# Broadcast of the reciprocal denominators in four transfers, three denominators computed inside the first gate/up, a third x1 buffer

## The chip, the cores and the metric

The kernel runs on one core of a Trainium2 chip, in one launch. The metric is the device time of one execution in microseconds, from three runs: median 884.3 us (880.92 to 885.51). A lower time is better. The profile shows one execution in detail: PE is TensorE (matmul; PEld is its weight load), DVE is VectorE, ACT is ScalarE, POOL is GpSimd, SP is SyncE, which here only issues DMAs.

## The reference

A transformer block in bf16 with S = 2048 tokens and D = 1024 features, conditioned by a vector c. `silu(c) @ w_mod` gives six vectors of 1024: shift, scale and gate for each of the two halves.

```python
h = layernorm(x) * (1 + ca) + sa
x = x + ga * A(h)             # linear attention, 32 heads of 32
h = layernorm(x) * (1 + cb) + sb
x = x + gb * B(h)             # silu(h @ w_gate) * (h @ w_up) @ w_down, F = 3584

# A: q, k, v = h @ wqkv
pq, pk = phi(q), phi(k)       # phi(t) = (t + 1 if t > 0 else exp(t)) + 1e-6
kv  = einsum('bhsd,bhse->bhde', pk, v);  z = sum of pk over s
num = einsum('bhqd,bhde->bhqe', pq, kv)
den = einsum('bhqd,bhd->bhq', pq, z) + 1e-6
A   = (num / den) @ wo
```

Because `kv` and `z` are sums over all tokens, no query can be finished before the keys of all tokens are done.

## The kernel before

The tokens are worked off in four chunks of 512 (`sc` = 0 to 3), each of four tiles of 128 rows. Features lie on the 128 partitions in eight groups of four heads (`hg`), so that q of one chunk is eight blocks of 128 x 512 (`q_phase(sc, lo, hi)`, one block `qc` each: eight matmuls into one accumulator, then `phi_to`: an Exp on ScalarE, L260, and two VectorE instructions, L261 and L262). The four accumulators `acc` (pool `pa`) are shared by q, k, v, gate/up and down.

The stages in order are: the first layer norm and k, v for all chunks, with q of chunk 0; then `kv` is masked to its head blocks and transposed (L471 to L481), and `wo` is multiplied by it in place (L485 to L492), so that later `pq @ wo` gives the attention output directly, provided that `pq` has been divided by its denominator. Between these stand the remaining q blocks. Then the four tiles of chunk 0 go through `wo_tile`, the q blocks that remain are done, and for each chunk follow `gate_up` (seven blocks `fb` of two 1 MB weight tiles `wgu`, four `f` each) and `down` (eight groups of 28 matmuls). `down` of chunk sc has the four `wo_tile` of chunk sc + 1 between its groups.

The denominators go through two functions. `den_norm(sc)` multiplies `pq` by `Zden` (32 small matmuls, L366 to L369), adds an epsilon and takes the reciprocal on VectorE (L371, L374), writes the 128 x 128 result to a DRAM scratch `rden_scratch` in four writes, two from ScalarE's queue and two from GpSimd's (L377), and reads it back from GpSimd's queue into the 1 MB tile `rbc`, each head's row copied to that head's 32 partitions (L380). `den_apply(sc)` multiplies `pq` by `rbc` in four VectorE instructions of two head groups (L388).

`wo_tile(st)` (L496 to L525) makes one tile of the residual stream x1: two halves of eight matmuls each (`a_ps`), the residual add (L513) and statistics (L514) on VectorE, a store of x1 to a DRAM scratch from ScalarE's queue (L515), rstd and a shift on GpSimd (L192, L206), the normalise on ScalarE (L208), and a transposing DMA from SP into `h2T` (L523). The fourth tile of a chunk is followed by eight `modulate` instructions on VectorE (L211). `down` loads x1 back in halves, `x1r`, from SP (L563), multiplies by the gate (L569), adds (L571) and stores (L572).

Who comes first on an engine is set by a planner that orders the traced instructions by its own estimates, with these exceptions: matmuls keep the order of the text (`keep_in_program_order`), and instructions under `tc.issue_after(i)` are queued on i's engine behind i (issue order only, no wait for i to finish). Every engine and every DMA queue works in order. SBUF tiles come from pools: a tile named in a pool of n buffers waits for the release of the one n before it; pool `k8` has 19 buffers of 8 KB per partition, which `rbc`, `wgu`, `wd`, `gu`, `pq`, `h2T`, `wq` and others share. Pool `x1p` holds two `x1` (4 KB) and three `x1r` (2 KB), pool `ep` three `e` (2 KB, used by gate/up and down) and three `eb`.

Of the kernel before, what the change touches and what calls it, by code (L numbers as in the profile page):

```python
# [9 lines left out]
ALU = mybir.AluOpType  # L10
BF16 = mybir.dt.bfloat16
F32 = mybir.dt.float32
# [9 lines left out]
def kernel(  # L22
# [13 lines left out]
    nc = tc.nc  # L36
    P = nc.NUM_PARTITIONS
    _, S, D = A_x.shape
    F = B_w_gate.shape[1]
    DH = 32  # L40
    HPC = P // DH
    ST = S // P
    DC = D // P
    HG = DC
    FC = F // P
    SCW = 512
    NSC = S // SCW
    STC = SCW // P
    NB = 512
# [19 lines left out]
    const = ctx.enter_context(tc.tile_pool(name="const", bufs=1))  # L69
    dram = ctx.enter_context(tc.tile_pool(name="dram", bufs=1, space=DRAM))  # L70
    k8 = ctx.enter_context(tc.tile_pool(name="k8", bufs=19))
    k2 = ctx.enter_context(tc.tile_pool(name="k2", bufs=5))
    x1p = ctx.enter_context(tc.tile_pool(name="x1p", bufs=2))
    ep = ctx.enter_context(tc.tile_pool(name="ep", bufs=3))
    yp = ctx.enter_context(tc.tile_pool(name="yp", bufs=2))
    small = ctx.enter_context(tc.tile_pool(name="small", bufs=4))
# [20 lines left out]
    def mm(out, lhsT, rhs, start, stop):  # L97
        return tc.keep_in_program_order(nc.tensor.matmul(out, lhsT=lhsT, rhs=rhs, start=start, stop=stop))  # L98
# [4 lines left out]
    def big(name, shape):  # L103
        return k8.tile([P] + shape, BF16, name=name, tag="k8")

    def acc_a():
        return pa.tile([P, NB], F32, name="acc", tag="pa")
# [21 lines left out]
    for b in range(2):  # L129
        ts = []  # L130
        for q in (1, 0):
            t = big("wme", [DC, NB])
# [31 lines left out]
    ca1T = const.tile([P, DC], F32, name="ca1T")  # L164
    sbT = const.tile([P, DC], F32, name="sbT")
    cb1T = const.tile([P, DC], F32, name="cb1T")
    ga_bc = const.tile([P, D], BF16, name="ga_bc")
    gb_bc = const.tile([P, D], BF16, name="gb_bc")
    kvs = k8.tile([P, HG * VW + HG * P], F32, name="kvs", tag="k8")
    kv_acc = kvs[:, 0:HG * VW].rearrange("p (g e) -> p g e", e=VW)  # L170
# [73 lines left out]
    def mod_block(b, q):  # L244
# [10 lines left out]
        else:  # L255
            nc.vector.tensor_copy(out=saT[:, cs], in_=src)

    def phi_to(dst, acc):
        e = ep.tile([P, NB], BF16, name="eb")
        nc.scalar.activation(out=e[:], in_=acc, func=ACT.Exp)  # L260
        nc.vector.tensor_scalar(out=e[:], in0=e[:], scalar1=1.0, scalar2=PHI_EPS, op0=ALU.min, op1=ALU.add)  # L261
        nc.vector.scalar_tensor_tensor(out=dst, in0=acc, scalar=0.0, in1=e[:], op0=ALU.max, op1=ALU.add)  # L262

    pks, vs, pqs = {}, {}, {}

# [33 lines left out]
    def q_phase(sc, lo=0, hi=DC):  # L299
        if lo == 0:  # L300
            pqs[sc] = big("pq", [HG, SCW])
        for qc in range(lo, hi):
            acc = acc_a()
            for cc in range(DC):
                mm(acc[:], lhsT=wq[cc // 4][:, cc % 4, qc * P:(qc + 1) * P], rhs=hTs[sc][:, cc, :],
                                 start=(cc == 0), stop=(cc == DC - 1))
            phi_to(pqs[sc][:, qc, :], acc[:])
# [55 lines left out]
    def den_norm(sc):  # L363
        pq = pqs[sc]
        den = acc_b("den")
        for hg in range(HG):  # L366
            for q in range(STC):
                mm(den[32 * q:32 * q + 32, 0:P], lhsT=Zden[:, hg, :], rhs=pq[:, hg, q * P:(q + 1) * P],
                                 start=(hg == 0), stop=(hg == HG - 1))  # L369
        dsum = small.tile([P, P], F32, name="dsum", bufs=2)  # L370
        nc.vector.tensor_scalar_add(out=dsum[:], in0=den[:, 0:P], scalar1=DEN_EPS)  # L371
        rb = small.tile([P, P], BF16, name="rb", bufs=2)
        with nc.allow_low_precision("bf16 reciprocal multiplies bf16 phi(q)"):
            nc.vector.reciprocal(out=rb[:], in_=dsum[:])  # L374
        for q in range(STC):
            eng = nc.gpsimd if q % 2 else nc.scalar
            eng.dma_start(out=rden_dram[sc, :, q * P:(q + 1) * P], in_=rb[32 * q:32 * q + 32, :])  # L377
        rbc = big("rbc", [HG, SCW])
        rv = rden_dram[sc].rearrange("(h g) t -> h (g t)", h=HPC)
        nc.gpsimd.dma_start(out=rbc[:].rearrange("p g t -> p (g t)"),  # L380
                            in_=rv.unsqueeze(1).to_broadcast([HPC, DH, HG * SCW]))
        rbcs[sc] = rbc

    def den_apply(sc):
        pq, rbc = pqs[sc], rbcs.pop(sc)
        for k in range(4):
            ks = slice(2 * k, 2 * k + 2)
            nc.vector.tensor_tensor(out=pq[:, ks, :], in0=pq[:, ks, :], in1=rbc[:, ks, :], op=ALU.mult)  # L388
# [51 lines left out]
    for sc in range(NSC):  # L440
        if sc > 0:
            k_phase(sc, 0, 2)
            kv_phase(sc - 1)
            if sc == 2:
                mod_bc(row)
            if sc == 3:
                mod_cols(row)
            k_phase(sc, 2, 8)
        v_phase(sc)
        if sc + 1 < NSC:  # L450
            with tc.issue_after(last_on[nc.vector.engine]):
                ln1(sc + 1)
                modulate_all(hTs[sc + 1], ca1T, saT)
        if sc == 0:
            q_phase(0)
        if sc + 2 < NSC:
            for st in range((sc + 2) * STC, (sc + 3) * STC):
                load_x(st, nc.sync)
        if sc == 1:
            row = mod_rows([2 * D, 2 * D + NB, 5 * D, 5 * D + NB])  # L460
        if sc == 2:
            row = mod_rows([3 * D, 3 * D + NB, 4 * D, 4 * D + NB])
            wo = load_w(wo_v, 0, "wo")
            for cc in range(DC):
                w = wo[cc // 4][:, cc % 4, :]
                nc.vector.tensor_tensor(out=w, in0=w, in1=ga_bc[:], op=ALU.mult)

    q_phase(1, 0, 2)
    kv_phase(NSC - 1)
    for h in range(2):  # L470
        hs = slice(4 * h, 4 * h + 4)  # L471
        nc.vector.tensor_tensor(out=KVZ[:, hs, :], in0=kv_acc[:, hs, 0:P],
                                in1=kvmask[:].unsqueeze(1).to_broadcast([P, 4, P]), op=ALU.mult)
        nc.vector.tensor_tensor(out=Zden[:, hs, :], in0=kv_acc[:, hs, P:P + 1].to_broadcast([P, 4, DH]),
                                in1=zmask[:, hs, :], op=ALU.mult)
# [4 lines left out]
    nc.scalar.copy(out=KVT[:, 0:4, :], in_=tpk[:, 0:4, :])  # L480
    nc.vector.tensor_copy(out=KVT[:, 4:8, :], in_=tpk[:, 4:8, :])  # L481
    den_norm(0)
    den_apply(0)
    q_phase(1, 4, 5)
    wf = [(hg, nb) for hg in range(HG) for nb in range(NNB)]  # L485
    for qc in range(5, 11):
        q_phase(1 + qc // 8, qc % 8, qc % 8 + 1)
        for hg, nb in wf[3 * (qc - 5):3 * (qc - 4)]:
            ps = acc_b("wf")
            w = wo[hg // 4][:, hg % 4, nb * NB:(nb + 1) * NB]  # L490
# [40 lines left out]
    def gate_up(sc, between=None):  # L531
        guT[sc] = []
        for fb in range(NFB):
            wb = []
            for view in (wg_v, wu_v):
                w = big("wgu", [DC, FBW])
                last_w[sc] = nc.sync.dma_start(out=w[:], in_=view[:, :, fb * FBW:(fb + 1) * FBW])
                wb.append(w)
            for fj in range(FPB):
                f = fb * FPB + fj  # L540
                if f % GPT == 0:
                    guT[sc].append(big("gu", [min(GPT, FC - f), SCW]))
                ps = []
                for w in wb:
                    acc = acc_a()
                    for cc in range(DC):
                        last_mm[sc] = mm(acc[:], lhsT=w[:, cc, fj * P:(fj + 1) * P], rhs=h2Ts[sc][:, cc, :],
                                              start=(cc == 0), stop=(cc == DC - 1))
                    ps.append(acc)
                sg = ep.tile([P, NB], F32, name="e")  # L550
                nc.scalar.activation(out=sg[:], in_=ps[0][:], func=ACT.Silu)  # L551
                gm = nc.vector.tensor_tensor(out=guT[sc][f // GPT][:, f % GPT, :], in0=ps[1][:], in1=sg[:], op=ALU.mult)  # L552
            if between and fb in between:
                with tc.issue_after(gm.ins):
                    between[fb]()

    def down(sc, side):
        for t in range(STC):
            st = sc * STC + t
            for nb in range(NNB):  # L560
                ns = slice(nb * NB, (nb + 1) * NB)
                x1r = x1p.tile([P, NB], F32, name="x1r", bufs=3)
                nc.sync.dma_start(out=x1r[:], in_=x1_dram[st * P:(st + 1) * P, ns])  # L563
                y_ps = acc_a()
                for f in range(FC):
                    mm(y_ps[:], lhsT=guT[sc][f // GPT][:, f % GPT, t * P:(t + 1) * P],
                                     rhs=wd[f // WDF][:, f % WDF, ns], start=(f == 0), stop=(f == FC - 1))
                yt = ep.tile([P, NB], F32, name="e")
                nc.vector.tensor_tensor(out=yt[:], in0=y_ps[:], in1=gb_bc[:, ns], op=ALU.mult)  # L569
                ob = yp.tile([P, NB], BF16, name="ob")  # L570
                nc.vector.tensor_tensor(out=ob[:], in0=yt[:], in1=x1r[:], op=ALU.add)  # L571
                nc.sync.dma_start(out=out2[st * P:(st + 1) * P, ns], in_=ob[:])  # L572
                if side:
                    with tc.issue_after(last_mm[sc].ins):
                        side.pop(0)()

    q_phase(2, 3, 4)
    den_norm(1)
    q_phase(2, 4, 5)
    for st in range(STC):  # L580
        wo_tile(st)
    q_phase(2, 5, 8)
    q_phase(3, 0, 5)
    den_norm(2)
    q_phase(3, 5, 8)
    def late_den():
        den_apply(2)
        den_norm(3)

    gate_up(0, {2: lambda: den_apply(1), 3: late_den, 5: lambda: den_apply(3)})  # L590
    wd = []
    for b in range(FC // WDF):
        w = big("wd", [WDF, D])
# [38 lines left out]
```

## Time and profile before

| | |
|---|---|
| median of three runs | 884.3 us |
| lowest, highest | 880.92, 885.51 us |
| profiled execution, time | 881.36 us |
| its span, first to last instruction | 879.6 us |
| TensorE busy | 840.3 us (96%) |
| VectorE, ScalarE, GpSimd busy | 306.7, 173.9, 37.0 us |
| mean granted TensorE clock | 0.986 of full |

The span is the time from the first to the last instruction of the profiled execution; its own time is 1.8 us more. The page has a strip in which each digit is the busy share of one of forty equal slices of 22 us. The chain of waits follows the last instruction back, step by step, to what released it. In the timeline a bracket behind an instruction gives the idle time before it on its engine and what ended it. Times "to landing" of a DMA run from its issue to its completion. A busy TensorE need not run at full clock: the granted clock of a stretch is given as a share of full speed.

### The profile page before, as it was taken

The page shows a single profiled execution, that of the slowest core. Times are in us where ns is not written, and L with a number is a line of the kernel's source. Part 1 is how long each engine was busy: PE and PEld are TensorE (multiplying, and loading weights), DVE is VectorE, ACT ScalarE, POOL GpSimd, SP SyncE. Part 2 cuts the span into 40 slices and gives each one's busy share as a digit, 9 for nine tenths or more (in the row PEclk, how much of TensorE's full clock was granted, in tenths as well). Part 3 has the DMA queues.
Part 4 walks back from the last instruction along what each step waited for, and adds up shares of the span by engine and source line. Part 5 has one row for each costly group of instructions (what it writes and reads, how often), then busy time and mean ns, then how long its engine had stood idle before and what let it go on. Part 6 is the DMA issues. An engine that isn't in the chain of part 4 may idle for free.

```text
span 879.6 us, 10369 instructions
## 1 busy us (share of the span) xinstructions
PE 840.3 (96%) x4201; PEld 387.4 (44%) x4284; DVE 306.7 (35%) x602; ACT 173.9 (20%) x267; POOL 37.0 (4%) x124
## 2 busy tenths in 40 slices
PE   9989999959599998999999999999999999999997
PEld 4434445524244443444444444444444444444443
DVE  5776334426531422443121134321212441212122
ACT  1555333342221121110111101011111101111100
POOL 2120000001000000000000000000000000000000
PEclk9999999989799999999999999999999999999999
DMA  9779530017995497552744226294321737820021
GB/s 298 288 156 296 182 121 1 2 49 96 251 296 160 145 185 237 171 150 91 222 142 138 103 80 216 69 289 135 121 96 42 216 91 247 267 96 1 7 66 36
DMA packets 127311, 128.74 MB, mean 146 GB/s; under 512 B 34976, under 2 KB 108832, under 8 KB 126752
## 3 DMA queue, kind: packets, MB, share of 16 engines
q1 hardware_dynamic: 122208, 115.36, 45.7%
q10 hardware_dynamic: 2688, 8.46, 2.5%
q0 software_dynamic: 2368, 4.27, 2.1%
q8 instruction: 33, 0.54, 0.3%
q14 instruction: 14, 0.11, 0.0%
HBM read 108.01 MB, written 12.71 MB: 137 GB/s over the span
## 4 chain that ended last, share of the span: by engine, by line
PE 82%; DMA 11%; DVE 4%; issue 1%; ACT 1%; POOL 1%; ACTq 0%; SPq 0%; DVEq 0%; POOLq 0%
PE acc L98 75%; DMA rbc<-rden_scratch 5%; PE a_ps L98 5%; DMA x1r<-x_scratch 2%; DMA wd<-in_B_w_down_dram 2%; DVE stats L198 1%; DVE pq L388 1%; DMA x_scratch<-x_2148 1%; DMA x_sb<-in_A_x_dram 1%; PE kvp L98 1%; DMA h2T<-xn 0%; DMA rden_scratch<-rb 0%; PE modr L98 0%; DVE pq L262 0%; ACT v L297 0%
## 5 line engine op out<-in xcount | busy, mean ns | idle before, releaser
L98 PE MATMUL acc<-h2T,wgu 128*128 128x512 bf16 x1757 | 385.9, 379 | 4.6 <-DVE gu L552 2.7
L98 PEld LDWEIGHTS <-wgu 128*128 128x128 bf16 x1792 | 175.3, 98 | 214.1 <-issue 3.0
L98 PE MATMUL acc<-wd,gu 128*128 128x512 bf16 x878 | 195.0, 379 | 3.0 <-DMA wd<-in_B_w_down_dram 2.1
L552 DVE TENSOR_TENSOR gu<-acc,e 128x512 bf16<-128x512 f32 x112 | 77.3, 691 | 294.3 <-PE acc L98 281.7
L551 ACT ACTIVATE e<-acc 128x512 f32<-128x512 f32 x112 | 66.9, 597 | 376.7 <-PE acc L98 358.9
L98 PEld LDWEIGHTS <-gu 128*128 128x128 bf16 x896 | 87.7, 98 | 108.1 <-issue 2.6
L98 PE MATMUL acc<-hT,wq 128*128 128x512 bf16 x248 | 62.3, 403 | 24.1 <-DVE pq L262 23.4
L98 PEld LDWEIGHTS <-hT 128*128 128x128 bf16 x512 | 49.6, 98 | 60.8 <-DVE hT L211 1.0
L569 DVE TENSOR_TENSOR e<-acc,gb_bc 128x512 f32<-128x512 f32 x32 | 22.1, 690 | 121.2 <-PE acc L98 112.8
L98 PE MATMUL a_ps<-wo,pq 128*128 128x512 bf16 x250 | 56.9, 379 | 0.3
L98 PE MATMUL acc<-wk,hT 128*128 128x512 bf16 x250 | 56.1, 379 | 0.3
L98 PE MATMUL acc<-wv,hT 128*128 128x512 bf16 x249 | 55.5, 379 | 0.4
L260 ACT ACTIVATE eb<-acc 128x512 bf16<-128x512 f32 x64 | 37.5, 596 | 75.6 <-PE acc L98 49.7
L98 PEld LDWEIGHTS <-wq 128*128 128x128 bf16 x256 | 26.0, 102 | 57.4 <-issue 31.1
L261 DVE TENSOR_SCALAR eb<-eb 128x512 bf16<-128x512 bf16 x64 | 18.4, 290 | 71.9 <-ACT eb L260 71.7
L98 PEld LDWEIGHTS <-pq 128*128 128x128 bf16 x256 | 25.0, 98 | 30.2
L192 POOL TENSOR_TENSOR rstd<-veps,neg_half 128x1 f32<-128x1 f32 x32 | 17.9, 558 | 449.7 <-DVE veps L190 449.7
L297 ACT CAST v<-acc 128x512 bf16<-128x512 f32 x32 | 18.7, 584 | 31.4 <-PE acc L98 30.3
L198 DVE BATCH_NORM_STATS2 stats<-x_sb 128x6 f32<-128x512 bf16 x32 | 20.6, 672 | 7.7 <-DMA x_sb<-in_A_x_dram 7.5
L571 DVE TENSOR_TENSOR ob<-e,x1r 128x512 bf16<-128x512 f32 x32 | 22.1, 692 | 1.1
L262 DVE SCALAR_TENSOR_TENSOR pk<-acc,eb 128x512 bf16<-128x512 f32 x32 | 22.1, 690 | 0.8
L262 DVE SCALAR_TENSOR_TENSOR pq<-acc,eb 128x512 bf16<-128x512 f32 x32 | 21.8, 686 | 0.7
(116 smaller groups left out, 251.0 us busy)
## 6 DMA issues: line engine op xcount, KB each, us to landing
wgu<-in_B_w_gate_dram SPq DMA_DIRECT2D x28, 1024.0 KB, 7.5
wgu<-in_B_w_up_dram SPq DMA_DIRECT2D x28, 1024.0 KB, 8.2
x_sb<-in_A_x_dram SPq DMA_DIRECT2D x32, 256.0 KB, 5.7
wml<-in_w_mod_dram SPq DMA_DIRECT2D x8, 1024.0 KB, 9.7
x1r<-x_scratch SPq DMA_DIRECT2D x32, 256.0 KB, 3.0
wd<-in_B_w_down_dram SPq DMA_DIRECT2D x7, 1024.0 KB, 28.7
wme<-in_w_mod_dram SPq DMA_DIRECT2D x4, 1024.0 KB, 11.2
rbc<-rden_scratch POOLq DMA_DIRECT2D x4, 1024.0 KB, 23.8
```

Of the source, the lines that this page charges most:

```text
L98: return tc.keep_in_program_order(nc.tensor.matmul(out, lhsT=lhsT, rhs=rhs, start=start, stop=stop))
L192: nc.gpsimd.tensor_tensor(out=rstd[:, 0:n], in0=veps[:, 0:n], in1=neg_half[:].to_broadcast([P, n]), op=ALU.pow)
L198: nc.vector.bn_stats(out=stats[:, i, :], in_=src[:, i * NB:(i + 1) * NB])
L260: nc.scalar.activation(out=e[:], in_=acc, func=ACT.Exp)
L261: nc.vector.tensor_scalar(out=e[:], in0=e[:], scalar1=1.0, scalar2=PHI_EPS, op0=ALU.min, op1=ALU.add)
L262: nc.vector.scalar_tensor_tensor(out=dst, in0=acc, scalar=0.0, in1=e[:], op0=ALU.max, op1=ALU.add)
L297: nc.scalar.copy(out=v[:, t, nb * 4:(nb + 1) * 4, 0:P], in_=acc[:].rearrange("p (g e) -> p g e", e=P))
L388: nc.vector.tensor_tensor(out=pq[:, ks, :], in0=pq[:, ks, :], in1=rbc[:, ks, :], op=ALU.mult)
L551: nc.scalar.activation(out=sg[:], in_=ps[0][:], func=ACT.Silu)
L552: gm = nc.vector.tensor_tensor(out=guT[sc][f // GPT][:, f % GPT, :], in0=ps[1][:], in1=sg[:], op=ALU.mult)
L569: nc.vector.tensor_tensor(out=yt[:], in0=y_ps[:], in1=gb_bc[:, ns], op=ALU.mult)
L571: nc.vector.tensor_tensor(out=ob[:], in0=yt[:], in1=x1r[:], op=ALU.add)
```

## The change

Four things are edited. The read of `rbc` becomes four DMAs of 32 partitions each, one per head of a group. `den_apply(0)` moves from before the wo folding to behind the phi of q block (2, 3), and the norms of chunks 1, 2 and 3 move into the first `gate_up`: norm 1 after block 0, apply 1 and norm 2 after block 2, apply 2 and norm 3 after block 4, apply 3 after block 6, the last. (Before, norm 1 stood after q block (2, 3), norm 2 after (3, 4), apply 1 after block 2, apply 2 and norm 3 after block 3, apply 3 after block 5.) The `x1` tile gets a third buffer and `x1r` gives one up. `ga_bc`, which is used only before the wo folding, lies in one of the three `e` tiles instead of a tile of its own.

```diff
-    x1p = ctx.enter_context(tc.tile_pool(name="x1p", bufs=2))
+    x1p = ctx.enter_context(tc.tile_pool(name="x1p", bufs=3))
...
-    ga_bc = const.tile([P, D], BF16, name="ga_bc")
+    ga_t = ep.tile([P, NB], F32, name="e")
+    ga_bc = ga_t[:].bitcast(BF16)
...
+    last_phi = [None]
+
     def phi_to(dst, acc):
...
-        nc.vector.scalar_tensor_tensor(out=dst, in0=acc, scalar=0.0, in1=e[:], op0=ALU.max, op1=ALU.add)
+        last_phi[0] = nc.vector.scalar_tensor_tensor(out=dst, in0=acc, scalar=0.0, in1=e[:], op0=ALU.max, op1=ALU.add)
...
         rv = rden_dram[sc].rearrange("(h g) t -> h (g t)", h=HPC)
-        nc.gpsimd.dma_start(out=rbc[:].rearrange("p g t -> p (g t)"),
-                            in_=rv.unsqueeze(1).to_broadcast([HPC, DH, HG * SCW]))
+        for h in range(HPC):
+            nc.gpsimd.dma_start(out=rbc[h * DH:(h + 1) * DH].rearrange("p g t -> p (g t)"),
+                                in_=rv[h].unsqueeze(0).to_broadcast([DH, HG * SCW]))
...
     den_norm(0)
-    den_apply(0)
     q_phase(1, 4, 5)
...
-                x1r = x1p.tile([P, NB], F32, name="x1r", bufs=3)
+                x1r = x1p.tile([P, NB], F32, name="x1r", bufs=2)
...
     q_phase(2, 3, 4)
-    den_norm(1)
+    with tc.issue_after(last_phi[0].ins):
+        den_apply(0)
     q_phase(2, 4, 5)
     for st in range(STC):
         wo_tile(st)
     q_phase(2, 5, 8)
-    q_phase(3, 0, 5)
-    den_norm(2)
-    q_phase(3, 5, 8)
-    def late_den():
-        den_apply(2)
-        den_norm(3)
-
-    gate_up(0, {2: lambda: den_apply(1), 3: late_den, 5: lambda: den_apply(3)})
+    q_phase(3)
+
+    def late_den(apply, norm):
+        if apply:
+            den_apply(apply)
+        if norm:
+            den_norm(norm)
+
+    gate_up(0, {0: lambda: den_norm(1), 2: lambda: late_den(1, 2), 4: lambda: late_den(2, 3),
+                6: lambda: den_apply(3)})
```

More of the change, by code (lines that the diff above doesn't have):

```diff
@@ L465 @@
                 w = wo[cc // 4][:, cc % 4, :]
-                nc.vector.tensor_tensor(out=w, in0=w, in1=ga_bc[:], op=ALU.mult)
+                nc.vector.tensor_tensor(out=w, in0=w, in1=ga_bc, op=ALU.mult)
     q_phase(1, 0, 2)
```

## The prediction

> **What bounds the kernel now.** The page's strip of forty slices comes first: it says where TensorE is not busy.
>
> ```profile
> PE   9989999959599998999999999999999999999997
> ```
>
> Two slices of 22 us at 5, the 9th (176 to 198 us) and the 11th (220 to 242), and a small dent in the 16th; everything from 355 us on is full. The busy-time view by stretches prices the gaps:
>
> ```profile
> 187.90:198.40 10.50, 0.10 (x5) 0.12 (x2) 3.50 (x7) 0.01 (x1) 0.00 (x0) 0.63 0.13 37
> 198.35:201.35 3.00, 2.78 (x8) 1.09 (x9) 2.86 (x8) 0.60 (x1) 0.00 (x0) 0.56 0.00 0
> 222.20:230.60 8.40, 0.04 (x2) 0.01 (x1) 3.40 (x9) 2.70 (x4) 0.82 (x2) 0.66 1.02 180
> 230.58:236.42 5.84, 5.83 (x16) 2.06 (x16) 2.64 (x8) 1.20 (x2) 0.00 (x0) 0.61 1.06 314
> 236.40:238.20 1.80, 0.07 (x2) 0.05 (x1) 1.80 (x6) 0.01 (x1) 0.00 (x0) 1.00 1.08 366
> 355.30:870.00 514.70, 512.23 (x2338) 233.30 (x2386) 145.72 (x242) 65.03 (x96) 9.81 (x24) 1.00 0.42 131
> ```
>
> The columns are the stretch, its length, busy time with instruction count of PE, PEld, DVE, ACT and POOL, the granted clock, DMA share and GB/s. After each long gap the clock is about 0.6 for some microseconds. After 355 us nothing is left to gain. So the question is who releases TensorE, which the timeline says at each restart, and the chain says why:
>
> ```profile
> 198.35 0.58 PE L98 MATMUL acc<-hT,wq 128*128 128x512 bf16 x1 [10.40 <-DVE pq L262]
> 230.58 5.83 PE L98 MATMUL acc<-hT,wq 128*128 128x512 bf16 x16 [8.36 <-DVE pq L262]
> 238.15 3.61 PE L98 MATMUL acc<-hT,wq 128*128 128x512 bf16 x16 [1.74 <-DVE pq L262]
> 342.47 5.34 PE L98 MATMUL acc<-h2T,wgu 128*128 128x512 bf16 x24 [2.68 <-DVE gu L552]
> 352.63 1.02 PE L98 MATMUL acc<-wd,gu 128*128 128x512 bf16 x4 [0.50 <-DMA wd<-in_B_w_down_dram]
> 355.22 1.02 PE L98 MATMUL acc<-wd,gu 128*128 128x512 bf16 x4 [1.57 <-DMA wd<-in_B_w_down_dram]
> ```
> ```profile
> 175.51 19.33 DMA rbc<-rden_scratch
> 194.87 2.50 DVE pq L388 x4
> ...
> 205.72 5.85 DMA x_scratch<-x_2148
> 211.59 15.71 DMA x1r<-x_scratch
> ...
> 230.37 4.26 DMA h2T<-xn
> ...
> 310.28 29.02 DMA rbc<-rden_scratch
> ```
>
> First gap: VectorE's four multiplies of `den_apply(0)` stand ahead of the phi work and wait for the 1 MB broadcast; TensorE runs out of its four accumulators. Second gap: ScalarE's queue stands at the fourth x1 store, which waits for an x1r load of 15.71 us, and the Exp work stands behind it. Third: `den_apply(3)` waits for a broadcast of 29.02 us. Why the loads of the second gap are so slow is read from the DMA view of 204 to 232 us, against the same transfers later (400 to 870 us, the last two lines):
>
> ```profile
> rbc<-rden_scratch POOLq DMA_DIRECT2D x1, 1024.0 KB, 22.0
> x1r<-x_scratch SPq DMA_DIRECT2D x3, 256.0 KB, 13.1
> h2T<-xn SPq DMA_TRANSPOSE x4, 8.8
> ...
> x1r<-x_scratch SPq DMA_DIRECT2D x25, 256.0 KB, 3.0
> h2T<-xn SPq DMA_TRANSPOSE x8, 3.3
> ```
>
> Broadcast 1 is in flight beside them for 22.0 us; the loads take 13.1 instead of 3.0, the transposes 8.8 instead of 3.3.
>
> **The change, part by part.** *Four transfers for one broadcast.* In the stretch where broadcast 0 is alone (176.9 to 194.9), the queue table gives
>
> ```profile
> q0 software_dynamic: 465, 1.05, 23.6%
> ```
>
> 23.6% of 16 engines is 3.8 engines at 60 GB/s: the one transfer, whose outermost dimension has four steps, occupies four. Each new one has 32 rows outermost. No row shows such a broadcast, so bounds: from below, a 1 MB weight load lands in 5.1 us at best; from above, the rate stays and three more issues come on top.
>
> ```profile
> L377 POOL DMA_DIRECT2D rden_scratch<-rb x8: 496/503/712, 172.5 to 308.0; - x8
> L380 POOL DMA_DIRECT2D rbc<-rden_scratch x4: 700/710/715, 175.5 to 310.3; - x4
> ...
> DMA to landing us min/median/max: 19.3/23.8/29.0
> ...
> DMA to landing us min/median/max: 5.1/7.9/28.4
> ```
>
> (The landing lines are of the broadcasts and of the weight loads wgu.) An issue costs POOL 0.50 to 0.71 us, so four take 2.0 to 2.8. I take the weight load's median plus three issues: 7.9 + 2.1 = 10.0, landing at 185.5; bounds 175.5 + 5.1 = 180.6 and 175.5 + 19.3 + 2.1 = 196.9. Behind them on POOL stands only the rstd of the first x1 tile, over 10 us later: nothing.
>
> *`den_apply(0)` behind the phi of q(2,3), `den_norm(1)` out of this place.* q(2,3) is the last block before the stall. Its matmuls run 1.89 us from 185.50; then Exp, min and phi, then four multiplies (2.50 us):
>
> ```profile
> 185.50 1.89 PE L98 MATMUL acc<-hT,wq 128*128 128x512 bf16 x8
> ...
> L260 ACT ACTIVATE eb<-acc 128x512 bf16<-128x512 f32 x64 | 37.5, 596 | 75.6 <-PE acc L98 49.7
> L261 DVE TENSOR_SCALAR eb<-eb 128x512 bf16<-128x512 bf16 x64 | 18.4, 290 | 71.9 <-ACT eb L260 71.7
> L262 DVE SCALAR_TENSOR_TENSOR pq<-acc,eb 128x512 bf16<-128x512 f32 x32 | 21.8, 686 | 0.7
> ...
> 356.25 3.45 PE a_ps L98 x16
> ```
>
> 187.4 + 0.6 + 0.3 + 0.7 and hand-overs is 189.1: later than 185.5, so the broadcast is hidden with 3.6 us to spare; without that cover, its lateness comes one to one. The multiplies end at 191.6. TensorE does q(2,4) until 187.4 + 1.7 = 189.1 (sixteen matmuls take 3.45) and then needs the scaled chunk 0. If each pair of head groups is released by its own multiply, the first tile's half ends at 192.0 where 190.8 was possible, 1.2 lost; if it waits for all four, 2.5. Value 1.9, no reason for either. It is shorter than the 2.68 us gap after which the clock stayed whole, so no cold matmuls. Term 1: 10.4, plus the slow clock (8 matmuls in 3.00 us instead of 1.72: 1.3), minus 1.9: **9.8 us**.
>
> *Broadcast 1 and 2 leave the x1 stage, third x1 buffer.* VectorE's longest wait for a free x1 buffer was 6.7 us, ScalarE's wait on the x1r load 10.6:
>
> ```profile
> ACT xn L208 <- DMA x1r<-x_scratch: 10.6, 1, 10.6
> DVE x_2263 L513 <- DMA x_scratch<-x_2187: 6.7, 1, 6.7
> ```
>
> With three buffers, tile 3 takes over the one of tile 0, whose store is issued three tiles (3 x 3.45 us of matmuls) earlier. With no broadcast beside them, loads take 3.0 and transposes 3.3. What is late next: the normalise of tile 3, then Exp of q(2,5). An earlier tile shows its price from the residual add to the end of the normalise, 208.45 to 212.58, 4.1 us:
>
> ```profile
> 208.45 0.69 DVE L513 TENSOR_TENSOR x_2187<-a_ps,x_sb 128x512 f32<-128x512 f32 x1 [0.26 <-PE a_ps L98]
> 211.34 1.24 ACT L208 ACTIVATE xn<-x_2187,nmr,rstd 128x1024 bf16<-128x1024 f32 x1 [2.19 <-POOL nmr L206]
> ```
>
> The eight half tiles end at 192.0 + 7 x 1.73 = 204.1, so Exp of q(2,5) starts at 208.3 and its phi ends at 210.0; four accumulators carry TensorE to 204.1 + 6.9 = 211.0. Covered, by 1.0. The last transpose lands at about 211.8 and the eight modulate instructions may sit ahead of a phi: I leave 0.5, bounds 0 and the present 1.7. Term 2: 8.4 + (5.84 - 3.45) + 1.7 - 0.5 = **12.0 us**.
>
> *Denominators 1 to 3 inside the first gate/up.* Each block of it is 64 matmuls, 13.8 us. Norm and apply now lie two blocks apart, 27.6 us; even the present 24 to 29 us would nearly fit, and 10 to 15 do. Term 3: the third gap, **2.7 us**. The 32 small matmuls of two norms (0.56 us each) move inside; net zero. Each norm puts two writes on ScalarE's queue behind the reciprocal, with SiLU behind them. One such place exists now:
>
> ```profile
> ACT e L551 <- DVE rb L374: 6.4, 1, 6.4
> 300.00:310.00 10.00, 9.95 (x76) 4.58 (x75) 5.14 (x9) 1.79 (x3) 1.00 (x2) 1.00 0.05 9
> ```
>
> SiLU waited 6.4 us and TensorE stayed at 9.95 of 10: the accumulators hide it. Cost 0; if not, 2.7 (the third gap) three times, 8 us.
>
> *`den_apply(3)` at the very end of gate/up.* It frees broadcast 3's buffer later, perhaps for the seventh `wd` load, which TensorE needs 24 matmuls (5.2 us) into the first down group. The last gate weights' buffer falls free 1.7 us before the end, and without a slow broadcast a load lands in 5.1 to 7.9. Of today's 2.1 us of `wd` waits I count half as gone. Term 4: **1.0 us**, bounds 2.1 and, if the load must wait for that buffer (3 us late) and takes 7.9, a loss of 3 + 7.9 - 5.2 - 2.1 = 3.6.
>
> *Two x1r buffers, `ga_bc` in a borrowed tile.* In down a load follows each group's `ob`; with two buffers it has about 10 us until its use and lands in 3.0. The borrowed `e` slot is idle until gate/up. Both 0.
>
> Sum: 9.8 + 12.0 + 2.7 + 1.0 = 25.5 us. The profiled execution took 881.36 us (span 879.6 and 1.8 around it): 855.9. The median of the three runs, 884.3, is 2.9 above the profiled one; I add half of that: **857.4**.
>
> **The rivals.** *A: the four transfers stay as slow as the one.* They are queued one behind the other and read the same 64 KB. For it: 60 GB/s is all the broadcast ever got. Against: 3.8 busy engines explain that rate. Landing 196.9 instead of 189.1 costs 7.8, 1.3 of clock return, the third gap stays: 25.5 - 11.8 = 13.7, so 869.2. The Trainium skill, in SBUF — State Buffer, "Door 1: The DMA port swizzle", says that 32 partitions reach 8 of 16 ports (189 GB/s at 1 MiB), and under "Can I just issue two DMAs to hit both halves?" that two such transfers serialize. By that figure 1 MB takes an estimated 5.5 us, still under the cover; no run here shows it yet, and it keeps A at an eighth.
>
> *B: the second gap moves to the h2T wait.* VectorE stands at the modulate, ahead of phi, while transposes still take 8.8 us, slowed now by stores and weight loads. For it: 4.26 us of the chain is that transfer. Against: 3.3 in every later chunk. Price (8.8 - 3.3) + 2.4 of slow clock: 7.9, so 865.3.
>
> *C: the planner's order undoes it*, the norms landing where VectorE or ScalarE still blocks as long: 884.
>
> *D, slower: x1r becomes the bound.* Its place is every one of the 32 down groups: a load can start only when the `ob` two groups back has ended, in SP's in-order queue behind weight loads. Fully exposed it is 3.0 + 0.4 of issue, 3.4 us a group; half of it is 54 us, 910. It decides from 25.5 / 32 = 0.8 us a group. Against: some 7 us of cover and three spare accumulators.
>
> **How the numbers follow.** Forecast 0.62, A 0.12, B 0.14, C 0.07, D 0.05. Half a percent, 4.4 us, is about what a measurement tells from no change here. Faster holds forecast, A and B, 0.88; C is the same, 0.07; D slower, 0.05. The forecast's own range is 853 (10.4 + 1.3 - 1.2, 12.5, 2.7 and 2.1 make 27.8, so 853.6, and the lowest run shown is 0.4 below the profiled one) to 862 (term 4 at its loss of 3.6). A and B take the range up to 870; at the low end I add 2 for a gap that I did not see.
>
> **What would show it.** Right: each broadcast piece landing within 10 us of the first issue, VectorE at L388 never waiting for it, TensorE's gaps before 230 us under 3 us with clock 1.00 throughout, x1r and h2T near 3 us, gate/up starting some 23 us earlier. Wrong: L388 waiting (A), h2T L211 ahead of a TensorE gap (B), a gap released by SiLU or `wd` in gate/up, or `ob` waiting for x1r (D).

## The result and the profile after

The changed kernel took 857.73 us (median of four runs, 856.37 to 858.9) against 882.61 us for the kernel before on the same chip (four runs, 879.92 to 885.51). The ratio is 0.9717, with a 95% interval from 0.9676 to 0.9758. The profiled execution took 856.37 us with a span of 854.5; the one of before took 881.36, so 25.0 us lie between the two traces.

The strip of TensorE's forty slices, and the granted clock under it, from the page of the changed kernel:

```profile
PE   9989999999999998999999999999999999999997
PEclk9999999999999999999999999999999999999999
```

The two slices at 5 are full. The dents left are the third slice, which was there before as well, and the 16th, and the clock stays at 90% or more in every slice.

The timeline of TensorE at the places where before stood still (start, length, then in brackets the idle time and its releaser):

```profile
189.84 14.50 PE L98 MATMUL a_ps<-wo,pq 128*128 128x512 bf16 x63 [0.61 <-DVE pq L392]
...
215.33 8.79 PE L98 MATMUL acc<-hT,wq 128*128 128x512 bf16 x39 [0.63 <-DVE pq L265]
223.96 13.98 PE L98 MATMUL acc<-h2T,wgu 128*128 128x512 bf16 x63
...
322.66 4.48 PE L98 MATMUL acc<-wd,gu 128*128 128x512 bf16 x20
327.60 0.81 PE L98 MATMUL acc<-wd,gu 128*128 128x512 bf16 x3 [0.46 <-DMA wd<-in_B_w_down_dram]
330.13 1.02 PE L98 MATMUL acc<-wd,gu 128*128 128x512 bf16 x4 [1.73 <-DMA wd<-in_B_w_down_dram]
```

The gaps of 10.4, 8.36 and 1.74 us are now 0.61 and 0.63, and the 2.68 us in gate/up is gone. The waits for `wd` are as long as before, 0.46 + 1.73 = 2.2 against 2.1, but not from the same cause, as shown below.

The same by stretches (stretch, length, busy time of PE, PEld, DVE, ACT, POOL, then clock, DMA share, GB/s): the first gate/up with the start of down, and everything behind the last `wd` wait.

```profile
223.96:327.20 103.24, 102.65 (x555) 46.98 (x564) 31.16 (x49) 18.60 (x30) 8.94 (x18) 1.00 0.71 211
331.16:845.00 513.84, 511.37 (x2335) 232.99 (x2381) 145.87 (x242) 65.04 (x96) 9.81 (x24) 1.00 0.43 132
```

The last row answers the row of before from 355.30 on, 514.70 long with 512.23 busy. The idle rest is 2.47 us in both: nothing was lost or won there. The whole gain lies ahead of it.

The broadcast itself. First VectorE's four multiplies and the issue of broadcast 0 in the timeline, then the broadcast's line with its landing times, over all four broadcasts and for broadcast 0 alone, then its queue in the DMA view of the stretch in which its packets run, 176.8 to 181.2 us:

```profile
175.61 2.00 POOL L384 DMA_DIRECT2D rbc<-rden_scratch  x4 [1.74 <-DMA rden_scratch<-rb]
189.10 2.49 DVE L392 TENSOR_TENSOR pq<-pq,rbc 128x1024 bf16<-128x1024 bf16 x4
```
```profile
L384 POOL DMA_DIRECT2D rbc<-rden_scratch x16: 492/497/539, 175.6 to 303.4; - x16
...
DMA to landing us min/median/max: 3.4/8.9/11.5
...
DMA to landing us min/median/max: 3.4/4.5/6.6
```
```profile
q0 software_dynamic: 175, 1.04, 105.3%
```

The multiplies carry no bracket: they waited for nothing. The four transfers moved 1.04 MB in 4.4 us and held all sixteen engines (packet times overlap, so a share can pass 100%), where the single transfer held 3.8 from 176.9 to 194.9. The last piece landed by 183.7, 6.6 us after its issue.

### The profile page after: what moved, and what is told of

Its sections match the earlier page's. It is cut to its first block, busy times and chain, and to the rows that moved or that the text cites. A ratio compares the mean times of both kernels' runs of the same rounds, so it can differ in the third digit from the quotient of the medians.

```text
span 854.5 us, 10400 instructions
## 1 busy us (share of the span) xinstructions
PE 837.3 (98%) x4201; PEld 386.4 (45%) x4284; DVE 307.5 (36%) x602; ACT 174.1 (20%) x267; POOL 42.1 (5%) x136
## 3 DMA queue, kind: packets, MB, share of 16 engines
q0 software_dynamic: 1024, 4.26, 2.2%
## 4 chain that ended last, share of the span: by engine, by line
PE 91%; DMA 4%; DVE 3%; SPq 1%; issue 1%; ACT 0%; POOL 0%; DVEq 0%; POOLq 0%
PE acc L98 82%; PE a_ps L98 6%; DMA wme<-in_w_mod_dram 2%; DMA wd<-in_B_w_down_dram 1%; DVE stats L199 1%; DMA x_sb<-in_A_x_dram 1%; PE kvp L98 1%; SPq L137 1%; PE modr L98 0%; PE wf L98 0%; DMA h2T<-xn 0%; DVE hT L212 0%; DVE h2T L212 0%; PE den L98 0%; SPq L133 0%
## 5 line engine op out<-in xcount | busy, mean ns | idle before, releaser
L98 PE MATMUL acc<-hT,wq 128*128 128x512 bf16 x249 | 58.5, 387 | 3.9 <-DVE pq L265 3.4
L209 ACT ACTIVATE xn<-x,nmr,rstd 128x1024 bf16<-128x1024 f32 x16 | 19.9, 1241 | 131.3 <-POOL nmr L207 131.3
L516 DVE TENSOR_TENSOR x<-a_ps,x_sb 128x512 f32<-128x512 f32 x32 | 22.1, 691 | 8.3 <-PE a_ps L98 7.6
L517 DVE BATCH_NORM_STATS2 stats<-x 128x6 f32<-128x512 f32 x32 | 22.2, 695 | 1.1
```

The source lines that it names most:

```text
L209: nc.scalar.activation(out=dst, in_=src, func=ACT.Identity, bias=nmr[:], scale=rstd[:, 0:1])
L516: nc.vector.tensor_tensor(out=x1[:, ns], in0=a_ps[:], in1=x_t[:, ns], op=ALU.add)
L517: nc.vector.bn_stats(out=stats[:, nb, :], in_=x1[:, ns])
```

## The experiments

The theory was the prediction's: three gaps, each closed by a part of the change of its own. The first rival gave everything to the split, the second to the order and the buffer. Each ratio below is to the kernel before on the same chip.

**The changed kernel with the single transfer.** The order of the norms and the third buffer stay.

```diff
-        for h in range(HPC):
-            nc.gpsimd.dma_start(out=rbc[h * DH:(h + 1) * DH]..., in_=rv[h].unsqueeze(0)...)
+        nc.gpsimd.dma_start(out=rbc[:]..., in_=rv.unsqueeze(1).to_broadcast([HPC, DH, HG * SCW]))
```

> The changed kernel with the broadcast as one transfer again; everything else as changed. My theory (the split is what makes the broadcast quick, and its lateness comes one to one): broadcast 0 lands near 195 us instead of 184, VectorE waits about 5.7 us at den_apply(0), TensorE loses that and about 1.3 us of slow clock, and the broadcasts inside gate/up take 20 to 29 us again, which costs 0 to 2.5 us at each of the three applies: 865 to 871 us. Rival (the order of the work did it, the split adds little): 857 to 860 us.

Measured: 894.11 us (891.2 to 895.41), ratio 1.0166 [1.0137, 1.0196]. It is 1.7% slower than the kernel before, and both expectations fell. TensorE's waits, VectorE's and ScalarE's, each in us in total, times and longest:

```profile
PE acc L98 <- DMA wd<-in_B_w_down_dram: 15.6, 6, 11.8
PE a_ps L98 <- DVE pq L391: 6.3, 1, 6.3
PE acc L98 <- ACT e L553: 5.8, 2, 3.1
...
PE acc L98 <- DMA wgu<-in_B_w_up_dram: 1.3, 2, 1.1
```
```profile
DVE pq L391 <- DMA rbc<-rden_scratch: 27.7, 4, 11.7
```
```profile
ACT e L553 <- DVE rb L377: 23.4, 2, 12.0
```

VectorE now waits for all four broadcasts. In gate/up an apply and the next norm stand side by side, so each late broadcast delays the next reciprocal; SiLU stands 12 us behind that on ScalarE, and the accumulators no longer cover it (2 x 3 us on TensorE). The delays add up until broadcast 3 and the weight loads behind it start so late that `wd` costs TensorE 11.8 us at once. Together these four waits are 29.0 us against 2.8 in the changed kernel; the two profiled times, 893.22 and 856.37, are 36.9 apart, and the rest of some 11 us goes with a granted clock of 0.90 between 250 and 360 us:

```profile
250.00:360.00 110.00, 89.33 (x440) 38.45 (x439) 25.51 (x39) 13.49 (x23) 3.40 (x6) 0.90 0.80 176
```

The second gap, though, is not there (0.65 us): with broadcast 1 out of the x1 stage, the same transfers land fast although the broadcast is still the slow one. From the DMA view of 195 to 235 us:

```profile
x1r<-x_scratch SPq DMA_DIRECT2D x2, 256.0 KB, 3.8
h2T<-xn SPq DMA_TRANSPOSE x4, 4.9
```

**The kernel before with the split alone.**

```diff
-        nc.gpsimd.dma_start(out=rbc[:]..., in_=rv.unsqueeze(1).to_broadcast([HPC, DH, HG * SCW]))
+        for h in range(HPC):
+            nc.gpsimd.dma_start(out=rbc[h * DH:(h + 1) * DH]..., in_=rv[h].unsqueeze(0)...)
```

> The kernel before with only the broadcast split in four. My theory: VectorE's wait at den_apply(0) falls from 14.9 to about 4 us, so that the first gap (10.4 us) shrinks to 0 to 1; broadcast 1 still runs beside the x1 stage but for some 8 instead of 22 us, so that the second gap (12.5 us with its slow clock) shrinks to 3 to 8; the third (2.7) goes: 862 to 868 us. Rival (the order did it): the gaps stay about as they were, 876 to 883 us.

Measured: 854.72 us (853.45 to 857.01), ratio 0.9723 [0.9691, 0.9755]: the whole gain of the change, with one of its four edits. Both expectations were too high.

> The kernel before with the split alone, a second time, beside the changed kernel. Theory: the split carries the whole gain and the moved norms and the third x1 buffer add nothing, so this run stands within 2 us of the changed kernel, 855 to 858. Rival: the moved norms cost something of their own (the 2.2 us of wd waits, which the split alone did not show), so this run is 2 to 4 us below the changed kernel in the same hour, 853.5 to 855.

Beside the changed kernel on one chip it took 854.11 us (853.29 to 856.8), ratio 0.9697 [0.9658, 0.9735]; the rival's number. Its TensorE timeline around the x1 stage, the DMA view of 195 to 235 us, and the longest of TensorE's waits:

```profile
215.34 3.61 PE L98 MATMUL acc<-hT,wq 128*128 128x512 bf16 x16 [1.06 <-DVE pq L262]
228.22 34.06 PE L98 MATMUL acc<-h2T,wgu 128*128 128x512 bf16 x154 [1.70 <-DVE pq L262]
```
```profile
rbc<-rden_scratch POOLq DMA_DIRECT2D x8, 256.0 KB, 7.0
...
x1r<-x_scratch SPq DMA_DIRECT2D x3, 256.0 KB, 6.5
h2T<-xn SPq DMA_TRANSPOSE x4, 3.5
```
```profile
PE acc L98 <- DVE pq L262: 5.0, 3, 2.2
```

Broadcasts 1 and 2 are still beside the x1 stage and the q blocks, but short: transposes take 3.5 us instead of 8.8, x1r loads 6.5 instead of 13.1, and of the second gap two waits of 1.06 and 1.70 us are left. The planner, too, puts the multiplies of `den_apply(0)` behind the phi of q(2,3) by itself, at 188.75 us in the first of these two profiles. TensorE does not wait for `wd` at all, in neither profile. So the second gap has two cures, and either is enough to take away most of it: a short broadcast (here) or the broadcast elsewhere (the run above). That run had the third x1 buffer too; the broadcast elsewhere with two buffers and one transfer was not run.

**The third buffer, taken away and given alone.**

```diff
-    x1p = ctx.enter_context(tc.tile_pool(name="x1p", bufs=3))       # changed kernel
+    x1p = ctx.enter_context(tc.tile_pool(name="x1p", bufs=2))
-                x1r = x1p.tile([P, NB], F32, name="x1r", bufs=2)
+                x1r = x1p.tile([P, NB], F32, name="x1r", bufs=3)
```

> The changed kernel with two x1 and three x1r buffers again. My theory: once no broadcast runs beside the x1 stage, a store lands 2.6 us after its issue, before the tile two later needs its buffer, so the third buffer is worth 0 to 0.5 us: 856.5 to 859 us. Rival (the third buffer opened the x1 stage): VectorE waits for the store again and the second gap comes back in part, 863 to 868 us.

Measured: 859.28 us (855.55 to 862.12), ratio 0.9772 [0.9737, 0.9807], 0.3 us above the theory's range. VectorE's longest wait for a free x1 buffer is then 0.4 us, and the second gap 1.10 us instead of 0.63. The other way round, the kernel before with this edit turned (and `ga_bc` in the borrowed tile):

> The kernel before with only the third x1 buffer, two x1r buffers and the borrowed tile. My theory: VectorE's 6.7 us wait for a store goes, but broadcast 1 still slows the loads and transposes beside it, so that the second gap stays within 4 us of its size: 878 to 883 us. Rival (the third buffer opened the x1 stage): the second gap goes, 869 to 874 us.

Measured: 880.49 us (877.68 to 883.37), ratio 1.0011 [0.9992, 1.0029]. Its gaps stay:

```profile
PE acc L98 <- DVE pq L263: 22.3, 4, 9.7
```

With the slow broadcast beside the x1 stage the third buffer cures nothing. In the changed kernel its trace gives it about half a microsecond; by the times the run without it is 1.6 and 2.6 us above the changed kernel's two medians, which were taken on other chips, with single runs that overlap, so that a worth of a few microseconds is not ruled out there.

**The move of `den_apply(0)` alone**, in the kernel before.

```diff
     den_norm(0)
-    den_apply(0)
...
     den_norm(1)
+    with tc.issue_after(last_phi[0].ins):
+        den_apply(0)
```

> The kernel before with only den_apply(0) moved behind the phi of q block (2, 3); one transfer, norms 1 to 3 and the x1 buffers as before. Theory: the broadcast still lands at 194.9, so the 10.4 us gap shrinks to the 6.3 us wait that the changed kernel with one transfer had at its first a_ps, and the second and third gap stay: some 4 to 6 us gained, 874 to 877 against 880 for the kernel before. Rival: the position alone frees the first gap (10 to 12 us gained): 868 to 870. Second rival: what is saved at the first gap is only moved into the second, and the time stays at 879 to 881.

Measured: 874.61 us (873.55 to 877.75), ratio 0.9933 [0.9911, 0.9956], 6.0 us below before's 880.66; as the theory had it. The first gap shrinks to the lateness of the broadcast, most of the second stays, and the third is 0.9 us instead of 2.7:

```profile
194.68 1.04 PE L98 MATMUL a_ps<-wo,pq 128*128 128x512 bf16 x2 [5.48 <-DVE pq L390]
...
226.03 9.86 PE L98 MATMUL acc<-hT,wq 128*128 128x512 bf16 x32 [7.32 <-DVE pq L264]
```

**Two transfers instead of four**, in the kernel before: is it the number of transfers that counts, or the steps of their outermost dimension?

```diff
+        for h in range(0, HPC, 2):
+            nc.gpsimd.dma_start(out=rbc[h * DH:(h + 2) * DH]...,
+                                in_=rv[h:h + 2].unsqueeze(1).to_broadcast([2, DH, HG * SCW]))
```

> The kernel before with the 1 MB broadcast as two transfers of 64 partitions, each with two steps in its outermost dimension; all else as before. Theory: a transfer is given as many engines as its outermost dimension has steps, so the two get two engines each, together the four of the single transfer; broadcast 0 lands 19 to 22 us after its issue (twice that if both fall on the same two engines), and the time is that of the kernel before, 877 to 884, or above 890 in the second case. Rival: smaller transfers land sooner because there are more of them, two in half the time, 10 to 13 us, and most of the gain of the split is there: 856 to 864.

Measured: 883.05 us (881.58 to 886.28), ratio 1.0032 [1.0009, 1.0054]. The landing times of its broadcasts, and the stretch of 177 to 189 us in the DMA view:

```profile
DMA to landing us min/median/max: 17.5/25.0/30.4
```
```profile
q0 software_dynamic: 99, 0.81, 24.6%
```

24.6% of sixteen is 3.9 engines for two transfers of two steps each, against 3.8 for one of four steps and sixteen for four of thirty-two. The steps count, not the number of transfers. The Trainium skill says this in DMA: Bandwidth & Descriptors, "Rules for kernel authors": an outermost dimension of fewer than 16 steps confines a DMA to that many engines at most. The trace agrees: 3.8 engines for four steps, 3.9 for two times two. A single transfer with more outermost steps was not run. The planner put `den_apply(0)` later here too, so that TensorE's gaps are others than before (5.2, 9.4 with 4.7, and 4.9 us), but about as long in sum.

**The `wd` wait.** It stayed at 2.2 us in the profile of the changed kernel and was 4.7 in a second one of it. SP's queue in the first (start, how long the group of issues took):

```profile
281.18 20.24 SPq L507 DMA_DIRECT2D x_sb<-in_A_x_dram  x4
301.51 19.98 SPq L600 DMA_DIRECT2D wd<-in_B_w_down_dram  x7
```
```profile
SPq L507 <- DMA rden_scratch<-rb: 13.3, 2, 12.9
```

The x loads of chunk 1 stand on SP until the write of norm 3 to the scratch has landed, and the weights behind them. Why an x load has to wait for that write the profile does not tell; the two share no tile. So the first `wd` load leaves 21.2 us ahead of the first down group (322.66), and the seventh lands 9.0 us after its issue:

```profile
321.12 8.97 DMA wd<-in_B_w_down_dram
```

In the kernel before the x loads stood there as well, and longer, but the first `wd` load still left 36.9 us ahead of the down group (310.79 and 347.64). SP's wait, and the issue and landing of that load:

```profile
SPq L504 <- DMA rden_scratch<-rb: 16.4, 2, 16.0
...
L594 SPq DMA_DIRECT2D wd<-in_B_w_down_dram x1: 379/379/379, 310.8 to 310.8; - x1
...
DMA to landing us min/median/max: 28.7/28.7/28.7
```

What made `wd` late there was the single transfer: this first load, issued 0.5 us behind broadcast 3, landed 0.2 us after it, and the chain to the seventh runs through that broadcast and `den_apply(3)`. The split alone has the same hold of 16.0 us on SP, sends its first `wd` load 34.0 us ahead of the down group (289.83 and 323.87) and has no `wd` wait. So the split took the old wait away, and the move of norm 3 brought a new one of the same size.

Two other orders were run on this, beside a second run of the changed kernel, and the first of them twice:

> The changed kernel once more, beside the split alone and beside an order with earlier norms. Theory: 857.5 us (856 to 859), with TensorE waits for wd of 2.2 us and no wait of more than 3 us. There is no rival for this run; it is the yardstick for the next two.

Measured: 856.66 us (855.44 to 861.01), ratio 0.9731 [0.9694, 0.9769].

```diff
-    gate_up(0, {0: lambda: den_norm(1), 2: lambda: late_den(1, 2), 4: lambda: late_den(2, 3),
-                6: lambda: den_apply(3)})
+    gate_up(0, {0: lambda: den_norm(1), 1: lambda: den_norm(2), 2: lambda: late_den(1, 3),
+                3: lambda: den_apply(2), 4: lambda: den_apply(3)})
```

> The changed kernel with norm 2 one block earlier (after block 1) and norm 3 two blocks earlier (after block 2), applies 1, 2 and 3 after blocks 2, 3 and 4. Theory: the wd loads are late because SP's queue stands at the x loads that wait for the write of norm 3 (20.24 us at 281.18), so with norm 3 some 28 us earlier the wd waits fall from 2.2 us to 0.5 or less and the time is 1.7 to 2.2 below the changed kernel: 855 to 856 if that gives 857.5. Rival: the seventh wd load waits for the buffer of the last gate weights whatever the norms do, wd waits stay at 1.5 to 2.5 and the time is that of the changed kernel within 1 us. Second rival: VectorE's applies wait again since only one block lies between norm 3 and the next apply; a SiLU wait without loss on TensorE up to 8 us, or a gap of 1 to 3 us and 858 to 860.

Measured on the chip of the run just told: 853.11 us (852.04 to 855.41), ratio 0.9685 [0.965, 0.972], without any `wd` wait, and 3.6 us below the changed kernel, where the theory had 1.7 to 2.2. From its SP queue:

```profile
276.99 3.04 SPq L507 DMA_DIRECT2D x_sb<-in_A_x_dram  x4
280.43 28.00 SPq L600 DMA_DIRECT2D wd<-in_B_w_down_dram  x7
```

Earlier norms also free the buffers of `rbc` earlier, so SP's order was tried by itself, with all norms where the change puts them:

```diff
-            with tc.issue_after(last_w[sc - 1].ins):
+            with tc.issue_after((last_wd[0] if sc == 1 else last_w[sc - 1]).ins):
                 nc.sync.dma_start(out=x_t[:], in_=x2[st * P:(st + 1) * P, :])
...
+        last_wd[0] = nc.sync.dma_start(out=w[:], in_=wd_v[:, b * WDF:(b + 1) * WDF, :])
```

> The changed kernel, all norms and applies in its places, with only one thing swapped: SP issues the seven wd loads ahead of the four x loads of chunk 1, so that no wd load stands behind the loads that wait for the write of norm 3. Theory: SP's order is what makes wd late, so the wd waits fall from the 2.2 and 4.7 us of the two profiles of the changed kernel to 0.5 or less, first wd issue before 290, and the time is 1.5 to 3.5 us below that kernel's 857.7 and 856.7: 853.5 to 855.5. Rival: the wd loads wait for buffers that apply 3, after the last block, frees late; the waits stay at 1.5 to 5 us and the time at 856 to 858. Second rival: the x loads, now behind the seventh wd, come late for the first x1 tile of chunk 1; a new wait of 2 to 6 us at its residual add, 858 to 862.

Measured: 852.49 us (851.58 to 853.5), ratio 0.9689 [0.9661, 0.9717], a little below the theory's range; no `wd` wait, clock 1.0, and the residual add of the first x1 tile waits for TensorE only. From its SP queue and TensorE's timeline:

```profile
278.96 40.16 SPq L601 DMA_DIRECT2D wd<-in_B_w_down_dram  x7
319.18 2.37 SPq L507 DMA_DIRECT2D x_sb<-in_A_x_dram  x4
```
```profile
320.29 6.21 PE L98 MATMUL acc<-wd,gu 128*128 128x512 bf16 x27
```

> The order with earlier norms once more, on the chip of the run with the wd loads first. Theory: 853 us (852 to 855.5), no wd wait, and level within 1.5 us with the run that has the wd loads first, since both take away the same wait. Rival: its lead over the changed kernel was chance, and it stands at 856 to 858.

Measured on the same chip: 853.19 us (851.32 to 853.49), ratio 0.9693 [0.9665, 0.9721]. The two are level, and each of their runs, on both chips, is below each run of the changed kernel (855.41 at the highest against 855.44 at the lowest); the run with the `wd` loads first had no changed kernel beside it on its chip. SP's order is the cause of the changed kernel's `wd` wait, and the buffers need no part in it. These have the lowest medians of the case, 3.5 to 5 us under the changed kernel's two and about 1 us under those of the split alone, whose runs overlap with theirs.

**Earlier norms with the single transfer**, to see whether lateness of norm 3 was also what made the first experiment so slow.

```diff
-        for h in range(HPC):                                        # earlier norms
-            nc.gpsimd.dma_start(out=rbc[h * DH:(h + 1) * DH]...)
+        nc.gpsimd.dma_start(out=rbc[:]...)
```

> The order with earlier norms (norms 1, 2, 3 after blocks 0, 1, 2, applies 1, 2, 3 after blocks 2, 3, 4), with the single transfer instead of four. Theory: the single transfer cost 894 in the changed kernel's order because norm 3 stood behind two slow broadcasts and SP's x loads and wd loads behind it (15.6 us of wd waits with the slow clock after them); with norm 3 two blocks earlier the wd waits fall to about 2 us, while the first wait of 6.3 us and the SiLU waits of 3 us each stay: 872 to 880. Rival: the single transfer disturbs the weight loads wherever it stands in gate/up, or broadcasts that now overlap share their four engines and take 40 us and more: 888 or above.

Measured: 880.45 us (875.29 to 882.9), ratio 0.9981 [0.996, 1.0001]; just above the theory's range, and by other waits than it named. The `wd` waits went, all of them, and so did SiLU's, but two new ones came:

```profile
PE acc L98 <- DVE gu L554: 11.5, 1, 11.5
PE a_ps L98 <- DVE pq L391: 6.1, 1, 6.1
PE acc L98 <- DMA wgu<-in_B_w_up_dram: 4.9, 1, 4.9
```
```profile
325.89 2.50 DVE L391 TENSOR_TENSOR pq<-pq,rbc 128x1024 bf16<-128x1024 bf16 x4 [16.20 <-DMA rbc<-rden_scratch]
```

VectorE stands 16.2 us at the last apply, with the gate/up multiplies behind it. So the late norm 3 does explain the `wd` waits of the first experiment, but with the slow broadcast TensorE waits in gate/up in both orders, 16.4 us here (11.5 + 4.9) and 22.7 there (15.6 + 5.8 + 1.3); what waits there changes.

## Why the prediction was right, and where it was not

The number, 857.4 against 857.73, and the mechanism of each gap held. The credit for the parts did not.

*The split.* Landing at 185.5 was forecast, bounds 180.6 and 196.9; the packets ended at 181.2 and the last piece landed by 183.7. The difference changed nothing, for the cover reaches to 189.1, as worked out: the multiplies start at 189.10. The later broadcasts took longer, up to 11.5 us for a piece, so the sign of 10 us did not hold for them, at no price: VectorE waits for none. By the Trainium skill, SBUF — State Buffer, "Door 1: The DMA port swizzle", 1 MB at 32 partitions was an estimated 5.5 us; the trace has 4.4, 236 GB/s instead of the 189 given there. The advice of the Trainium skill there, under "Can I just issue two DMAs to hit both halves?", that only one transfer over all partitions reaches every port, speaks against a split; here the measurement goes the other way: the one transfer, with its four outermost steps, was the slow form.

*The wait at a_ps* was put at 1.9, with 1.2 if each multiply releases its own pair. The first eight matmuls take 2.41 us instead of 1.89, behind a gap of 0.61:

```profile
189.84 2.41 PE L98 MATMUL a_ps<-wo,pq 128*128 128x512 bf16 x8 [0.61 <-DVE pq L392]
```

That is a loss of 1.1 (0.61 and 0.52), near the 1.2 of a release in pairs. Term 1 was 0.8 too small. The clock stayed whole behind it, as forecast, but the 2.68 us gap that this was argued from is no safe bound (see the end).

*Term 2* left 0.5 and 0.63 is there. But it was credited to the third buffer and the departure of broadcasts 1 and 2. The buffer alone cured nothing, and the departure is one of two cures, of which the split, made anyway, is the other. The transfers of the x1 stage are not at 3 us, as the signs had it, but at 4.1 (x1r) and 4.9 (h2T) in the changed kernel; that was fast enough.

*Term 3* is right: the 2.68 us gap is gone. SiLU stands behind the reciprocals twice at no price, 102.65 of 103.24 us busy in that stretch; the 8 us bound of that cost is what the first experiment came near (5.8), where SiLU waited 12 us instead of 6.4.

*Term 4* failed: 1.0 was counted and 0 came. The step took half of before's wait as gone. With the split alone all of it goes, but the move of norm 3 brings a new one. For that the step looked in buffers and landing times and passed over SP's queue, where the `wd` loads stand behind the x loads that wait for norm 3. The change moves norm 3 from block 3 to block 4, so that the first `wd` load leaves 21.2 us ahead of its use instead of 36.9. The seventh was issued 1.5 us before the end of gate/up, about as worked out, but behind the other late loads it landed in 9.0 us, not in 5.1 to 7.9; with the `wd` loads first on SP it lands in 5.6. That run shows SP's order to be the cause.

*The sum*: 10.6, 11.9, 2.7 and 0 make 25.2; measured 25.0. Gate/up starts at 223.96 instead of 247.44, 23.5 us earlier, where some 23 were forecast. The two errors of 0.8 and 1.0 cancelled, which is luck. The half of 2.9 us that was added for the way from the profiled execution to the median had no reason but three runs; the median came out 1.4 above the profiled one.

*The rivals.* A fell with the landing times; the two-transfer run shows, in the order of before, how it would have looked. (The scratch of a chunk is 32 KB, four writes of 8.0, not the 64 KB that A gives; nothing hangs on it.) B fell: the gap before gate/up is 0.63, and the transpose in the chain takes 3.21 us (from 208.60) where it took 4.26.

C did not happen. D fell: no VectorE instruction waits for x1r, and the rows of down are unchanged.

What the prediction did not ask is whether the parts add up. They do not: the split alone gains 25.2 and 26.6 us in its two runs (879.91 to 854.72, 880.66 to 854.11), the rest adds nothing to it, and by the medians on one chip takes 2.5 us back, about what the `wd` wait is long; without the split, the rest loses 14 us (879.91 to 894.11). The prediction's rival A, which has all moves and the slow transfer, was priced at 869.2 and is 894: it counted only the lateness at the first apply and the third gap, and not the chain from apply to norm to SiLU and `wd` (5.8 and 15.6 us).

## What to carry to other kernels

When a transfer is long, count its engines before moving work around it (share x 16 in the queue table, for a stretch in which its packets run throughout): a form that uses more engines can make the moves needless. Work that is placed to hide a slow transfer is only as good as that transfer; two places in which one lands late in a row can cost more than the wait that was hidden. A load that lands late may simply have been issued late: read the issuing queue's own waits, and what stands ahead in it.

## What was not expected of the hardware

A broadcast that holds 3.8 of sixteen engines, with 19 to 32 us to its landing, slows its neighbours more than four short transfers that hold all sixteen. In the x1 stage, beside the single transfer, transposes took 8.8 us and x1r loads 13.1; beside the four short ones, 3.5 and 6.5; without a broadcast, in the changed kernel, 4.9 and 4.1. The bytes are the same. A load issued just behind a single transfer landed with it: in the kernel before the first `wd` load 0.2 us after broadcast 3 (28.7 us to landing), in the changed kernel with one transfer the second one 0.1 us after it (32.1 us), and this is the load that ended TensorE's wait of 11.8 us. That fits loads that queue on those few engines, but no run tells that from another cause.

The clock can fall after short waits, where they come close together. In the second profile of the changed kernel three `wd` waits of 1.2 to 1.8 us lie within 7 us; in the third the granted clock falls to 0.50 for 6.8 us, so that four matmuls take 1.86 us instead of 1.02, and the sixteen of a_ps 5.49 instead of 3.62:

```profile
326.76 1.02 PE L98 MATMUL acc<-wd,gu 128*128 128x512 bf16 x4 [1.20 <-DMA wd<-in_B_w_down_dram]
329.47 0.81 PE L98 MATMUL acc<-wd,gu 128*128 128x512 bf16 x3 [1.69 <-DMA wd<-in_B_w_down_dram]
332.11 1.86 PE L98 MATMUL acc<-wd,gu 128*128 128x512 bf16 x4 [1.83 <-DMA wd<-in_B_w_down_dram]
333.77 5.49 PE L98 MATMUL a_ps<-wo,pq 128*128 128x512 bf16 x16
...
330.70:337.50 6.80, 5.39 (x13) 1.87 (x13) 1.46 (x3) 0.00 (x0) 0.00 (x0) 0.50 0.14 39
```

That execution took 861.01 us, the longest of the six. In the changed kernel's two profiles the `wd` waits were 2.2 and 4.7 us in all; the two orders without them are 3.5 to 5 us faster by the medians.

A single wait can do it too, and the same wait does not always. The prediction took a gap of 2.68 us as harmless, and behind that one the clock was 1.00. But in the changed kernel with one transfer single waits of 3.05 and 2.74 us, for SiLU, were each followed by 3.3 us at a granted clock of 0.50. And in the third slice, ahead of all that the change touches, TensorE waits 2.1 to 2.9 us in every trace of the case. Here is what came behind that wait in the second run with earlier norms and in the second run of the split alone:

```profile
57.08 7.07 PE L98 MATMUL acc<-hT,wq 128*128 128x512 bf16 x31 [2.54 <-DVE pq L265]
```
```profile
57.28 8.75 PE L98 MATMUL acc<-hT,wq 128*128 128x512 bf16 x31 [2.23 <-DVE pq L262]
```

The longer wait left the clock whole and the shorter one cost 1.7 us. So waits of this length are a chance of a loss, and no length between 2.2 and 2.7 us divides the harmless from the others here. What decides it was not measured.
